# Row-tiled scores, a new beginning and copied global rows in a windowed attention with MLP

## The chip, the core and the metric

The kernel runs on one core of one Trainium2 chip. The metric is device time in microseconds of one execution; the profile beside it comes from one profiled execution of the same program. The engines are called by the profile's short names: PE (TensorE, with PEld for its weight loads), DVE (VectorE), ACT (ScalarE), POOL (GpSimd) and SP (SyncE, here a queue of transfers).

## The reference

Eight batches of eight heads, 576 positions, head size 64. A query sees the keys within 32 positions of its own, and eight positions are global: they see all keys, and all queries see them. The result of the attention, laid out as 4608 tokens of 512, goes through an MLP with h times cos(h) between its two matrices.

```python
scores = scale * np.matmul(q, k.transpose(0, 1, 3, 2))
mask = np.abs(pos[:, None] - pos[None, :]) <= window        # window = 32
mask = mask | is_global[:, None] | is_global[None, :]
scores = np.where(mask, scores, -1000000000.0)
attn = np.exp(scores - np.max(scores, axis=-1, keepdims=True))
attn = attn / (np.sum(attn, axis=-1, keepdims=True) + 1e-09)
attn_out = np.matmul(attn, v)
x = attn_out.transpose(0, 2, 1, 3).reshape(B * S, H * D)     # 4608 x 512
h = x @ w_in                                                 # w_in 512 x 2048
out = (h * np.cos(h)) @ w_out                                # w_out 2048 x 512
```

## The kernel before

**Tiling.** The attention works on pairs of heads: 32 pairs, four to a batch. The 576 queries of a pair are cut into 11 blocks (`NB`) of 56 (`QB`). For a block the kernel holds 128 keys in `kw`: the 8 global ones in rows 0 to 7 and a window of 120 local ones; and 64 queries in `qb`: the 8 global ones and the block's 56. Head 0 of the pair lies in partitions 0 to 63, head 1 in 64 to 127. In `qb` each head has a slot of its own, zero in the other head's partitions, so that one matmul over all 128 partitions gives both heads' scores side by side.

The steps of a pair, by the letters with which the program writes its order:

- `k`, `q` (`local_k`, `local_q`): bring keys and queries into `kw` and `qb`. For the first eight pairs PE turns them from rows (`turned`, L492), and ACT and DVE copy them out of PSUM (L499, L512); from pair 8 on they come turned by a transfer from an fp16 copy in DRAM, and DVE lays them out (L502, L515).
- `g` (`globals_k`, `globals_q`): POOL copies the global keys and queries in (L479, L483, L484). They come from `kgT` and `qgT`, made at the start from gathered rows (`gather`, `build_globals`, L442, L464, L465).
- `s` (`scores`, L525 to L528), in three groups of 4, 4 and 3 blocks: matmuls `st`, exp on ACT to `e`, product with the mask on DVE to `pm`.
- `w` (`spread`, L370, L374, L377), first eight pairs only: PE spreads rows of v over the blocks' windows by matmuls with shifted identities (`shift`), and the global rows of v with `own`; each block takes its global rows first, then one or two shifted parts. ACT and DVE copy the result to `vw`. Later pairs get `vw` from transfers (`load_v`, `load_vg`). `C` (`cast_vn`, L348 to L351) casts half a batch of v's rows to fp16 before its two pairs are spread.
- `p` (`values`, L537 to L548): 22 matmuls into one PSUM tile `pv`, then reciprocals of the denominators and the product `xn` on DVE.
- `x` (`turn_x`, L560 to L568): six transposes, and copies into `xT`, the MLP's input; with the last pair of a batch POOL puts the global queries' rows in place.

The MLP runs in units: `1` is one `ph` (four matmuls of 512 columns, L578), its cos on ACT (L584) and its product g on DVE (L585); `2` is four matmuls of 512 columns into `po` (L595), four of which make an output tile that ACT or DVE copies out. `m` is the matmul part of a `1` alone, `t` its ACT and DVE part. `n` (L614) sums squares for a check, on ACT.

**Order.** All engines work in program order, and the order is written out by hand. First comes a straight beginning (memsets, index rows, masks, the loads of the first q and k). Then `FRONT` runs pairs 0 to 7 with hardly any MLP. Then 13 turns (s = 3 to 15) do the attention of two pairs (`a`, `z`) beside eight `1` and eight `2`, after `ORDER`, with `MID` in place of it in the first turn and small variants in the next three. A tail does the rest of the MLP. Letters `L`, `W`, `O`, `K`, `B`, `A`, `c` issue transfers: halves of q and k, w_in, w_out, fp16 copies, turned q and k with v, the later gathers, v's fp16 copy.

**Queues.** POOL issues the loads that change type (q, k, w_in, w_out, fp16 copies) and the gathers; SP issues v's rows (24 loads by `load_vn`), the turning transfers, `load_v`, `load_vg`, the later gathers and the output.

**PSUM.** Eight banks: `s` three (scores, spread, and outside the front the transposes of x), `h` two (ph; in the front the turned q and k), `o` one (po; in the front the transposes of x), `pv` two. A wait for a bank is a wait for the last reader of what was in it.

Of the kernel before, what the change touches and what calls it, by code (L numbers as in the profile page):

```python
# [19 lines left out]
P = 128  # L20
# [20 lines left out]
ORDER = "sa0 sa1 sa2 2 2 2 sz0 2 sz1 sz2 pa 1 1 2 xa pz G 1 1 2 xz n 1 1 2 kc qc 1 kd qd 2 1"  # L41
# [3 lines left out]
FOURTH = "2 2 sa0 sa1 sa2 2 sz0 2 sz1 sz2 pa 1 1 2 xa pz G 1 1 2 xz n 1 1 2 kc qc 1 kd qd 2 1"  # L45

FIFTH = "sa0 sa1 sa2 2 2 2 sz0 2 sz1 sz2 pa 1 2 xa pz G 1 2 xz n 1 2 kc qc 1 kd qd 2"

SIXTH = "sa0 sa1 sa2 2 2 2 sz0 2 sz1 sz2 pa 1 1 2 xa pz G 1 1 2 xz n 1 1 D0 2 kc qc D1 1 kd qd D2 2 1"

FRONT = ("s0.0 s0.1 s0.2 k1 q1 C0 w0 s1.0 s1.1 s1.2 L2 p0 k2 q2 C1 w1 x0 s2.0 s2.1 s2.2 W0 p1 k3 q3 C2 w2 x1 "
         "s3.0 s3.1 s3.2 L3 W1 A g4 g5 p2 k4 q4 w3 x2 s4.0 s4.1 s4.2 g6 g7 c4 K4 W2 W3 p3 k5 q5 C3 w4 x3 s5.0 s5.1 s5.2 p4 k6 q6 w5 x4 n0 "
         "s6.0 s6.1 s6.2 K5 p5 k7 q7 w6 x5 B4 s7.0 s7.1 s7.2 O p6 w7 n1 x6 m p7 m x7 t t")
# [145 lines left out]
def kernel(  # L199
# [51 lines left out]
    qb = [keep.tile([P, 2, NB, C], FP16, name=f"qb{i}") for i in range(NK)]  # L251
# [33 lines left out]
    d_i = keep.tile([P, C], I32)  # L285

# [37 lines left out]
    shift = xT[:, 0, 4 * TT : 5 * TT].rearrange("p (a n) -> p a n", n=P)  # L324
    own = xT[:, 1, 4 * TT : 6 * TT].rearrange("p (a n) -> p a n", n=P)
# [13 lines left out]
    def hold(pr):  # L339

        nc.gpsimd.tensor_copy(gate, qb[pr % NK][0:1, 0, 0, G : G + 1])
# [11 lines left out]
    def build_shifts():  # L353
# [5 lines left out]
        nc.vector.tensor_copy(own[:, :, 0:G], ident16[:, 0 : 8 * G].rearrange("p (b g) -> p b g", g=G))  # L359

    def spread(pr):

        new, h0 = vn16(pr // 2), 2 * (pr % 2) * D
        for g0 in range(0, NB, 4):
            n = min(4, NB - g0)
            t = ps.tile([P, 4, P], FP32, tag="s", bufs=3)
            for j in range(g0, g0 + n):
                i = j // 2
                parts = ((2, i), (3, i + 1)) if j % 2 else ((0, i), (1, i - 1))
                nc.tensor.matmul(t[:, j - g0], own[:, pr], vg16[:, 0].rearrange("p h d -> p (h d)"), start=True, stop=False)  # L370
                parts = [(a, x) for a, x in parts if x >= 0]
# [14 lines left out]
    mask = keep.tile([P, NB, 2, C], FP16)  # L386

    def build_mask():
# [26 lines left out]
        for h in range(2):  # L415
            nc.vector.tensor_tensor(
                mask[:, :, h, G:], view(nk, (1, NB), (0, QB)), view(band[:, G:], (0, NB), (1, QB)), ALU.mult)
            nc.vector.tensor_scalar(
                mask[:, :, h, 0:G], view(val, (1, NB), (0, G)), own[:, 0:1], None, ALU.mult)
# [11 lines left out]
        for h in range(2):  # L431
            nc.vector.tensor_copy(mask[0:G, :, h, G:], view(one, (0, NB), (0, QB)))
# [5 lines left out]
    def build_globals(half):  # L438
        both = []
        for src, dst in ((kg32, kgT), (qg32, qgT)):  # L440
            g16 = work.tile([P, P], FP16, tag="g16")
            nc.scalar.copy(g16, src[:, half].rearrange("x h d -> x (h d)"))  # L442
# [422 lines left out]
```

## Time and profile before

| | us |
|---|---|
| median of 3 runs | 369.73 |
| range of the runs | 367.13 to 370.02 |
| the profiled execution: its own time | 371.58 |
| the profiled execution: span from first to last instruction | 369.8 |

Mean granted PE clock over the span 0.988. Busy shares of the span: PE 91%, PEld 50%, DVE 72%, ACT 67%, POOL 29%.

A row of the profile names the source line, the engine, the operation, output and inputs, the shape, and how many there were; then busy time and mean duration of one, and the idle time just before it with what ended it. The chain of waits follows the work that ended last back through whatever released it; "issue" there is time in which an engine waited for nothing that the profile shows. Starts of matmuls in a row overlap their ends, so the distance from one group's start to the next one's start is the time that a group costs PE, and not its printed duration.

### The profile page before, as it was taken

What the parts mean: (1) busy time and instruction counts of PE and PEld (TensorE: products, weight loads), DVE (VectorE), ACT (ScalarE), POOL (GpSimd) and SP (SyncE); (2) the same over time, 40 slices, a digit from 0 to 9 for tenths busy, and PEclk for the clock granted to TensorE, in tenths of its full rate; (3) what the DMA queues carried; (4) which work ended last, traced back from release to release, by engine and by line L of the source; (5) the groups of instructions that cost most, each with busy time, mean ns of one, the idle gap of its engine ahead of it and who ended that gap; (6) DMA issues with size and microseconds to landing.
All of it is one profiled execution on the core that took longest, in us unless ns stands there. A gap on an engine that the chain in (4) does not pass through costs nothing.

```text
span 369.8 us, 8014 instructions
## 1 busy us (share of the span) xinstructions
PE 335.9 (91%) x2934; PEld 184.9 (50%) x2934; DVE 266.3 (72%) x615; ACT 249.5 (67%) x384; POOL 105.9 (29%) x239
## 2 busy tenths in 40 slices
PE   0399883999998999999999999999999999999992
PEld 0277673545553545555555555555555444444441
DVE  7659974696888888888888888888878445455410
ACT  5488882679776677778777868677787756644300
POOL 6735670161335250705253252603000100000000
PEclk9999997899999999999999999999999999999999
DMA  5979999999999999999999999999920000100111
GB/s 92 197 129 159 180 165 107 198 176 147 102 161 105 194 126 195 125 169 138 195 161 159 160 142 165 160 202 118 130 59 31 28 30 28 57 30 28 53 64 65
DMA packets 176280, 45.57 MB, mean 123 GB/s; under 512 B 164937, under 2 KB 171337, under 8 KB 176041
## 3 DMA queue, kind: packets, MB, share of 16 engines
q1 hardware_dynamic: 112601, 27.61, 58.3%
q0 software_dynamic: 63632, 17.37, 50.3%
q8 instruction: 25, 0.41, 0.5%
q14 instruction: 22, 0.18, 0.2%
HBM read 45.07 MB, written 20.05 MB: 176 GB/s over the span
## 4 chain that ended last, share of the span: by engine, by line
PE 79%; DVE 6%; issue 5%; ACT 3%; POOL 3%; DMA 2%; POOLq 0%; ACTq 0%
PE po L595 32%; PE ph L578 30%; PE st L525 5%; PE pv L537 4%; PE tx L560 2%; PE t L374 2%; DMA qn<-in_q_dram 2%; DVE g L585 2%; ACT e L527 1%; PE t L370 1%; PE t L492 1%; PE pn L628 1%; DVE xn L548 1%; POOL q L262 1%; ACT qb L512 1%
## 5 line engine op out<-in xcount | busy, mean ns | idle before, releaser
L584 ACT ACTIVATE cos<-ph,pio 128x512 f16<-128x512 f32 x144 | 97.1, 687 | 66.3 <-PE ph L578 64.7
L595 PE MATMUL po<-w_out,g 128*128 128x512 f16 x576 | 141.6, 379 | 0.0
L578 PE MATMUL ph<-xT,w_in 128*128 128x512 f16 x576 | 140.1, 379 | 0.3 <-DVE g L585 0.2
L585 DVE TENSOR_TENSOR g<-cos,ph 128x512 f16<-128x512 f16 x144 | 95.9, 685 | 46.9 <-ACT cos L584 44.9
L595 PEld LDWEIGHTS <-g 128*128 128x128 f16 x576 | 55.2, 98 | 62.1
L578 PEld LDWEIGHTS <-w_in 128*128 128x128 f16 x576 | 53.6, 98 | 60.5 <-issue 1.3
L527 ACT ACTIVATE e<-st 128x512 f16<-128x512 f32 (+1 forms) x96 | 47.9, 561 | 15.5 <-PE st L525 9.4
L528 DVE TENSOR_TENSOR pm<-e,mask 128x512 f16<-128x512 f16 (+1 forms) x96 | 37.2, 405 | 22.8 <-ACT e L527 21.0
L752 POOL COPY gate<-xn 1x1 f16<-1x1 f16 x12 | 2.2, 181 | 132.3 <-DVE xn L548 132.3
L525 PE MATMUL st<-qb,kw 128*128 128x128 f16 x352 | 29.2, 223 | 9.4 <-issue 5.0
L525 PEld LDWEIGHTS <-kw 128*128 128x128 f16 x352 | 24.1, 100 | 19.8 <-issue 9.1
L548 DVE TENSOR_TENSOR xn<-pv,r_all 128x768 f16<-128x768 f32 x32 | 30.7, 958 | 1.7
L568 POOL COPY xT<-xg 128x4 f16 x64 | 19.6, 306 | 28.7 <-DVE xT L563 25.3
L262 POOL DMA_DIRECT2D q<-in_q_dram x12 | 26.2, 2181 | 0.0
L614 ACT ACTIVATE sq<-xn 128x1536 f16<-128x1536 f16 x16 | 23.6, 1476 | 0.0
L515 DVE COPY qb<-qT 64x616 f16<-64x616 f16 x48 | 22.1, 460 | 0.3
L374 PE MATMUL t<-xT 112*128 112x128 f16 (+1 forms) x168 | 21.1, 240 | 0.7 <-ACT xT L349 0.4
L600 ACT COPY o<-po 128x512 f32<-128x512 f32 x18 | 10.5, 586 | 15.5 <-PE po L595 15.1
L262 POOL DMA_DIRECT2D k<-in_k_dram x12 | 19.8, 1646 | 0.0
L370 PE MATMUL t<-vg,xT 128*128 128x128 f16 x88 | 18.4, 242 | 0.9 <-issue 0.6
L537 PE MATMUL pv<-vw,pm 128*64 128x65 f16 x704 | 18.5, 199 | 0.0
L602 DVE COPY o<-po 128x512 f32<-128x512 f32 x18 | 12.3, 685 | 6.9 <-PE po L595 6.9
(123 smaller groups left out, 326.8 us busy)
## 6 DMA issues: line engine op xcount, KB each, us to landing
out_dram<-o SPq DMA_DIRECT2D x36, 256.0 KB
vw<-v SPq DMA_DIRECT2D x35, 165.0 KB
v<-in_v_dram POOLq DMA_DIRECT2D x12, 288.0 KB, 4.3
k<-in_k_dram POOLq DMA_DIRECT2D x12, 288.0 KB, 9.2
q<-in_q_dram POOLq DMA_DIRECT2D x12, 288.0 KB, 15.8
vn<-in_v_dram SPq DMA_DIRECT2D x20, 112.0 KB
w_in<-in_moe_w_in_dram POOLq DMA_DIRECT2D x4, 512.0 KB, 12.3
w_out<-in_moe_w_out_dram POOLq DMA_DIRECT2D x1, 2048.0 KB
```

What stands on the lines that cost most here:

```text
L262: nc.gpsimd.dma_start(dst[s].rearrange("t (h d) -> t h d", h=4), dview(src, base, (D, S), (S * D, 4), (1, D)))
L374: nc.tensor.matmul(t[:, j - g0], shift[0:m, a], new[0:m, x, h0 : h0 + 2 * D], start=False, stop=(a, x) == parts[-1])
L525: nc.tensor.matmul(st[:, j], kp[:, g0 + j], view(qp[:, :, g0 + j], (NB * C, 2), (1, C)), start=True, stop=True)
L527: nc.scalar.activation(e[:, :n], st[:, :n], AF.Exp, scale=scale)
L528: nc.vector.tensor_tensor(view(pm[:, g0], (1, n * P)), view(e, (1, n * P)), view(mask[:, g0], (1, n * P)), ALU.mult)
L537: nc.tensor.matmul(pv[r0 : r0 + C, j // 6, c0 : c0 + 65], pm[:, j, h], vp[:, j, h], start=True, stop=True)
L548: nc.vector.tensor_tensor(view(xn, (384, 2), (D, 6), (1, D)), view(pv, (512, 2), (65, 6), (1, D)), view(rp, (6, 2), (1, 6), (0, D)), ALU.mult)
L578: nc.tensor.matmul(ph, w_in16[:, j, f * P : (f + 1) * P], xT[:, j, t * TT : (t + 1) * TT], start=(j == 0), stop=(j == NC - 1))
L584: nc.scalar.activation(cos, ph, AF.Sin, bias=pio2)
L585: nc.vector.tensor_tensor(g, cos, ph, ALU.mult)
L595: nc.tensor.matmul(po, g16[:, f, s * P : (s + 1) * P], w_out16[:, f], start=(f == 0), stop=(f == NF - 1))
L614: nc.scalar.activation(sq, view(xn, (1, 2 * BP * P)), AF.Square, accum_out=x_sq[:, s : s + 1])
```

## The change

What it does:

- **Scores in row tiles.** `qb` loses its two zero-padded slots and holds both heads in their own partitions. Each block takes two matmuls, one on partitions 0 to 63 and one on 64 to 127, of 64 columns each, in alternation, into two PSUM banks. A whole pair is one step: blocks 0 to 7 of the two heads go into two banks, blocks 8 to 10 into two more; of the four, three have tag `s` and one `h` (in the front `o`). There are four exps (512, 512, 192, 192 columns) and three mask products. `pm` and the mask are laid out by head, and the mask has one copy for both heads. In the orders `sa0 sa1 sa2` become `sa`, and the second pair's groups, which stood around the fourth `2`, become one `sz` behind it.
- **Values.** The 22 matmuls alternate between the two column halves at every step.
- **Local queries** are copied by one instruction over 128 partitions instead of two over 64: in the front on ACT for pair 0 and odd pairs, on DVE for the others.
- **Beginning.** For pairs 0 and 1 the global keys and queries come from matmuls of the loaded rows with one-hot columns (`build_ones`, `pick_globals`), copied by ACT; the gathered rows of q and k are turned later, in two steps `H`. `warm` issues 7, 2 and 2 matmuls of identity with identity. Half of the memsets of the first k and q tiles move from DVE to ACT; v's rows are loaded only after a DVE memset that follows the index work; v's gather and the second load of q and k are issued before the gathers of k and q; `cast_vn(0)` moves into the beginning, ahead of the first scores; the memsets of `pv`, `kT` and `qT` come behind it.
- **Global rows of v.** For pairs 2 to 7 transfers copy them into spare rows of the tiles that get spread (`load_rows`), where the shifted identities have eight more rows for them; only pairs 0 and 1 still use `own`, once per group of blocks. Blocks that take the same shift go in one matmul of several columns' width.
- **Front.** Its steps are reordered, four units of ph are done in it instead of two, some with a third bank, and the transposes of x use tag `s`.

The core of the diff:

```diff
-ORDER = "sa0 sa1 sa2 2 2 2 sz0 2 sz1 sz2 pa 1 1 2 xa pz G 1 1 2 xz n 1 1 2 kc qc 1 kd qd 2 1"
+ORDER = "sa 2 2 2 2 sz pa 1 1 2 xa pz G 1 1 2 xz n 1 1 2 kc qc 1 kd qd 2 1"
...
+FRONT = ("s0 k1 i1 q1 j1 L2 w0 s1 k2 H0 C1 w1 H1 g2 g3 q2 p0 s2 W0 k3 q3 x0 C2 w2 p1 s3 L3 W1 A g4 g5 k4 q4 x1 w3 p2 "
+         "s4 g6 g7 c4 K4 W2 W3 k5 q5 x2 C3 w4 p3 s5 k6 q6 x3 w5 p4 s6 K5 k7 q7 x4 w6 p5 s7 B4 O w7 x5 n0 p6 + m m x6 p7 t t m m x7 t t n1 -")
+WARM = (7, 2, 2)
...
+    def build_ones():
+        gl = view(gidx_all, (0, RW), (2, G))
+        nc.vector.tensor_tensor(one_q, view(tok_i, (1, RW), (0, G)), gl, ALU.is_equal)
+        nc.vector.scalar_tensor_tensor(one_k, view(tok_i, (1, RW), (0, G)), float(-KPAD * RW), gl, ALU.add, ALU.is_equal)
+
+    def pick_globals(pr, src, ones, n, to):
+        t = ps.tile([P, G], FP32, tag="s", bufs=3)
+        for r in range(RW):
+            for h in range(2):
+                nc.tensor.matmul(t[h * D : (h + 1) * D], src[:n, 2 * pr + h, r], ones[:n, r], start=r == 0, stop=r == RW - 1)
+        nc.scalar.copy(to[:, :, 0:G], view(t, (0, NB), (1, G)))
+
+    def warm(n):
+        t = ps.tile([P, 4, P], FP32, tag="s", bufs=3)
+        for _ in range(n):
+            nc.tensor.matmul(t, ident16, view(ident16, (0, 4), (1, P)), start=True, stop=True)
...
+    def load_rows(s):
+        for pr in (2 * s, 2 * s + 1):
+            h0 = 2 * (pr % 2) * D
+            nc.sync.dma_start(vn16(s)[VT : VT + G, 0 : NVT - 1, h0 : h0 + 2 * D],
+                              view(vg16[pr * G : (pr + 1) * G, 0], (0, NVT - 1), (1, 2 * D)))
...
     def spread(pr):
...
-                nc.tensor.matmul(t[:, j - g0], own[:, pr], vg16[:, 0].rearrange("p h d -> p (h d)"), start=True, stop=False)
-                for a, x in parts:
-                    m = min(VT, S - VT * x)
-                    nc.tensor.matmul(t[:, j - g0], shift[0:m, a], new[0:m, x, h0 : h0 + 2 * D],
-                                     start=False, stop=(a, x) == parts[-1])
...
+            for n0, (a, j, k, x) in enumerate(runs):
+                m = min(VT, S - VT * x)
+                if m == VT and a in (0, 2, 4) and not first:
+                    m += G
+                nc.tensor.matmul(view(t[:, j], (2 * P, k), (1, P)), shift[0:m, a], new[0:m, x : x + k, h0 : h0 + 2 * D],
+                                 start=n0 == 0 and not first, stop=n0 == len(runs) - 1, skip_group_check=True)
...
-    def scores(pr, g):
-        for j in range(n):
-            nc.tensor.matmul(st[:, j], kp[:, g0 + j], view(qp[:, :, g0 + j], (NB * C, 2), (1, C)), start=True, stop=True)
...
+    def scores(pr):
+        kp, qp = kw[pr % NK], qb[pr % NK]
+        pm = pm_of[pr] = work.tile([P, 2, NB, C], FP16, tag="pm", name="pm")
+        tags = (("s", 3), ("s", 3), ("s", 3), ("o", 1) if front[0] else ("h", 2))
+        st = [ps.tile([P, 512], FP32, tag=tag, bufs=bufs, name="st") for tag, bufs in tags]
+        for j in range(NB):
+            for h in range(2):
+                hp = slice(h * D, (h + 1) * D)
+                nc.tensor.matmul(st[j // 8 * 2 + h][:, j % 8 * C : j % 8 * C + C], kp[hp, j], qp[hp, j], start=True, stop=True)
         for h in range(2):
+            e = work.tile([P, 512], FP16, tag="e", bufs=3)
+            nc.scalar.activation(e, st[h], AF.Exp, scale=scale)
+            nc.vector.tensor_tensor(view(pm[:, h], (1, 512)), e, view(mask, (1, 512)), ALU.mult)
+        e = work.tile([P, 512], FP16, tag="e", bufs=3)
+        n = (NB - 8) * C
+        for h in range(2):
+            nc.scalar.activation(e[:, h * n : (h + 1) * n], st[2 + h][:, 0:n], AF.Exp, scale=scale)
+        nc.vector.tensor_tensor(view(pm[:, 0, 8], (NB * C, 2), (1, n)), view(e, (n, 2), (1, n)), view(mask[:, 8], (0, 2), (1, n)), ALU.mult)
...
+        nc.scalar.activation(x_sq[:, 0:1], pio2, AF.Exp)
+        index_rows()
+        build_ones()
+        nc.vector.memset(vn32[0][0:1, 0, 0:1], 0.0)
         for s in range(2 * SB):
             load_vn(s)
+        gather(v, vg32, 0)
+        load_qk(1)
         gather(k, kg32, 0)
         gather(q, qg32, 0)
-        gather(v, vg32, 0)
...
+        warm(WARM[0])
         local_k(0)
+        pick_globals(0, kn[0], one_k, KP, kw[0])
+        warm(WARM[1])
         local_q(0)
-        build_globals(0)
+        pick_globals(0, qn[0], one_q, QP, qb[0])
         nc.scalar.copy(vg16[:, 0], vg32[:, 0])
-        for pr in range(4):
-            globals_k(pr)
-            globals_q(pr)
+        for s in range(1, 2 * SB):
+            load_rows(s)
+        cast_vn(0)
+        warm(WARM[2])
```

More of the change, by code (lines that the diff above doesn't have):

```diff
@@ L250 @@
     kw = [keep.tile([P, NB, P], FP16, name=f"kw{i}") for i in range(NK)]
-    qb = [keep.tile([P, 2, NB, C], FP16, name=f"qb{i}") for i in range(NK)]
+    qb = [keep.tile([P, NB, C], FP16, name=f"qb{i}") for i in range(NK)]
     def cast_half(s, which):
@@ L383, in load_vg @@
                 view(vg16[(pr % 16) * G : (pr % 16 + 1) * G, pr // 16, h], (0, NB), (1, D)))
-    mask = keep.tile([P, NB, 2, C], FP16)
+    mask = keep.tile([P, NB, C], FP16)
     def build_mask():
```

145 lines of the change are left out of this document (73 added, 72 removed).

## The prediction

> **What bounds the kernel now.** I read first the page's slices, then busy time by stage.
>
> ```profile
> PE   0399883999998999999999999999999999999992
> DVE  7659974696888888888888888888878445455410
> 56.00:64.00 8.00, 2.54 (x39) 2.04 (x39) 2.68 (x6) 2.06 (x5) 0.00 (x0) 0.80 1.66 103
> 72.00:80.00 8.00, 7.94 (x38) 3.52 (x36) 7.89 (x17) 5.63 (x9) 4.38 (x17) 1.00 1.37 194
> 150.00:200.00 50.00, 50.00 (x419) 26.69 (x418) 42.71 (x99) 38.00 (x58) 19.60 (x46) 1.00 1.61 163
> ```
>
> The columns of the last three are window, length, PE, PEld, DVE, ACT, POOL, clock, DMA share, GB/s. From 72 us on PE never rests (50.00 of 50.00), so there only its own work counts; before that it is idle a good part of the time, most of all at 56 to 64. The kernel is thus a front of 72 us with other limits, and a PE-bound rest. Next the chain of waits at that hole, and PE's timeline in one turn of the steady loop (start, us):
>
> ```profile
> 56.92 0.33 PE st L525 x3
> 57.25 5.04 issue
> 62.29 1.01 PE st L525 x8
> ```
>
> ```profile
> 158.00 0.39 PE L525 MATMUL st<-qb,kw 128*128 128x128 f16 x4
> ...
> 159.09 0.55 PE L525 MATMUL st<-qb,kw 128*128 128x128 f16 x7
> 159.57 0.57 PE L537 MATMUL pv<-vw,pm 128*64 128x65 f16 x22
> 160.07 1.90 PE L578 MATMUL ph<-xT,w_in 128*128 128x512 f16 x8
> ...
> 171.72 0.78 PE L525 MATMUL st<-qb,kw 128*128 128x128 f16 x11
> 172.33 0.59 PE L595 MATMUL po<-w_out,g 128*128 128x512 f16 x2
> ```
>
> In the hole PE stops in the middle of the 11 matmuls of one step and waits for nothing recorded; the DMA share is 1.66, and one 16 KB instruction fetch lies in it. Last the engines' rows by form (count, busy us, mean ns):
>
> ```profile
> L527 ACT ACTIVATE e<-st 128x512 f16<-128x512 f32 x64 | 36.0, 596 | 15.5 <-PE st L525 9.4 <-DVE pm L528 5.9
> L527 ACT ACTIVATE e<-st 128x384 f16<-128x384 f32 x32 | 15.8, 492 | 0.0
> L515 DVE COPY qb<-qT 64x616 f16<-64x616 f16 x48 | 22.1, 460 | 0.3
> L512 DVE COPY qb<-t 64x616 f16<-64x616 f16 x7 | 5.6, 803 | 1.6 <-ACT qb L512 1.5
> ```
>
> **The steady loop (13 turns of 16.92 us).** A turn is 8 ph and 8 po groups (0.863 each: 13.8), 22 score blocks, two value steps, two transposes. Eleven blocks take 172.33-171.72 = 0.61, so 55.6 ns a block. New are 22 matmuls of 64 columns, two per block in the two row halves. If halves overlap, a block takes half, 28 ns: 0.31 a step; if not, 0.61 as now. No row shows row halves, but the column halves of the value step are near: 22 matmuls of 65 columns in 160.07-159.57 = 0.50, the change to ph included, 23 ns each, where one alone needs 28. They overlap, so I take 0.32 and save 0.29 a step, 0.58 a turn.
>
> Against it: changing the shape of the tile costs time. From the seven st to pv are 0.48, seven blocks are 0.39, so 0.09. The scores now have a shape of their own: into and out of the first score step, and into the second (its way out is a change already): 3 x 0.09 = 0.27 back. PE nets -0.3 a turn. The new order in the value step saves nothing: its halves overlap now.
>
> What is late next: the scores take four PSUM banks, one of them from ph's two, and the second step's 11 blocks all stand behind the fourth po, where four stood before it. From the rows, exps are 0.49 apart at 512 columns and (596-492)/128 = 0.8 ns a column cheaper below, so 512, 512, 192, 192 spread over 0.49+0.49+0.23+0.34 = 1.55 from the step's first 16 matmuls. Laid out over a turn: two changes, 0.32 and four po put the second step at 4.06; its exps run from 4.42 to 5.97 (now, by the same layout, to 5.62), so the mask products end at 6.35, reciprocals and xn at 7.81; the table load (1.28) ends at 7.2 and cos and g follow every 0.6. The second ph would start at 5.83 and waits for the bank of the last exp, 0.16; the first transpose would start at 7.71 and waits for xn, 0.11; a later ph, at 11.67, waits for a g that DVE had to put behind the second xn, 0.17: +0.44. The same layout of the kernel before gives no wait, as the trace has it. DVE gives back one 0.46 copy a step (128x616 at once), which is cover only. Turn: 16.92-0.30+0.44, about 17.0, so +1.1 over 13 turns. Ends: no stall, -3.9; no overlap, where the same layout gives 17.53, +8.
>
> **The front.** From s2 (28.76) to s7 (56.92) a pair takes 5.63, with 0.96 and 0.59 of empty PE waits in these five. Sums per pair: DVE 1.23 masks, 1.53 reciprocals and xn, 0.80 q copy, 0.69 vw, 0.67 turned x, 0.44 cast: 5.36. ACT 1.47 exps, 1.26 k copy, 0.67 q copy, 1.07 vw, 0.31 cast: 4.78. PE about 4.4, of which spread takes 36.41 to 38.61, 2.2 for 32 matmuls. So DVE leads. The transfers do not: from 24 to 26 us the queues are nearly empty, since the third k, q load waits for PE (24.91), and in the steady loop PE never waits for one.
>
> Spread sheds its 11 matmuls of globals (but for one per group in two pairs) and runs its 21 others as 14 longer ones: 21 x 0.056 = 1.2. PE falls to about 3.3 a pair, but it isn't the limit: what counts is the q copy, one of 128x616 at the same 0.80 or 0.67, on DVE in three pairs of eight and on ACT in five. DVE 4.87, ACT 4.61 plus the early globals; I take 5.0 a pair.
>
> Start: DVE sheds one mask half (0.82+0.26+0.46), the two qb memsets (1.3) and half of kn's and qn's (0.9), and gains about 1.2 of one-hot and shift building; its mask is ready near 12 rather than 13, which hides under v's rows. Now s0 runs at 16.72, behind gathers, casts and POOL's copies, and s1 at 23.89, slowed by a cold PE (11 blocks in 1.17 at 16.72: 106 ns each). After, k and q load without the v loads beside them (those wait for DVE's index work, about 5.9, instead of 2.57), one-hot matmuls replace the gathers on this path, and identity matmuls (11 x 0.43 cold, under the wait for kn) warm PE. But the cast of v's first half now stands in ACT's and DVE's queues ahead of the first exps, and with it everything waits for v's rows. Now they are last seen needed at 19.13; six loads started 3 us later with less beside them I put at 16, between 12 and 20. Behind it on ACT: cast 0.62, exps 1.55, k copy 1.26, pick 0.27, q copy 0.67, pick 0.27 = 4.6, so s1 near 21. POOL now issues v's gather and the second k, q load first, and SP's queue gains six small copies ahead of the late gathers; first use is 10 us on, cost nothing, 0.5 each if that cover goes.
>
> Then six pairs of 5.0 bring s7 to 51. From s7 to the last turned x are now 72.45-56.92-5.04 = 10.5 without the hole; after, 1.6 of cold spread goes and two more ph groups (1.7) come in, so 61.5. Empty waits for instructions were 6.6 in all (5.04, 0.96, 0.59); the number of PE instructions is about the same, w_out is still loading, so I keep 3 (0 to 7): 64.5. Against 72.45: -8; and two ph groups less are left for later: -1.7.
>
> **Sum.** -8-1.7+1.1 = -8.6. The profiled execution took 371.58 around its span of 369.8: 363.0; it lay 1.85 over the median of 369.73, so 361.
>
> **Rivals.**
> 1. Everything pays (22%): v's rows at 13 (-3), no new instruction wait (-3), no stall in the loop (-3.9 instead of +1.1): 350 to 356, 353. For it: 0.44 of stalls hangs on margins of 0.1 to 0.4.
> 2. Row halves don't overlap (11%): 28 ns a matmul, turn 17.53, +8 instead of +1: 368. No row here excludes it. The Trainium skill, "TensorE: Matmul & The Clock Gate", section "Wait — 56ns, not 53.3ns?", says that matmul starts never come closer than about 25 ns; by that figure a step would take 0.55 and the sum would be about 367. The trace speaks against it: the value step has 22 in 0.50 with a change of shape in it, and the turns of k and q show 31 in 0.59, 19 ns each.
> 3. The front doesn't shrink (7%): v's rows at 19 again, and an instruction wait of 5 or more with w_out: -2-1.7+1.1, 367 to 370, 369.
> 4. Slower (8%): a row half's weights (still 128 columns) occupy PE as long as a whole block does now, and the halves' loads don't overlap: 55.6 ns a matmul, 1.22 a step, +0.61 twice, 0.27 and 0.2 of waits, 1.7 a turn, +22: 382. For it: PEld of L525 shows 100 ns a load; against: value loads hide at 23 ns each. It decides from about 37 ns a matmul: at 28 the kernel stands at 368, and each ns adds 44 x 13 = 0.57.
>
> **How the numbers follow.** Forecast 52%, 361, itself 355 to 367. 1% is 3.7 us, about what a measurement here tells from no change: faster is under 366.0, slower over 373.4. Faster: 48 of the 52, 22, 3 of rival 2, 1 of rival 3: 74%. Same: 4, 7, 5: 16%. Slower: 8, and 1 each of rivals 2 and 3: 10%. The range runs from 351 (a third of rival 1 outside) to 369 (rival 4, half of 3 and some of 2 outside).
>
> **What would show it.** Steady turn: score steps in about 0.32 plus 0.09 at each end, turn 16.7 to 17.1; over 17.4 means no overlap. Front: s1 near 21, pairs near 5.0, first stretch of unbroken ph near 64; the first cast of v waiting for a DMA. The number is wrong if one instruction wait in the front exceeds 7 us, or if ph shows waits over 0.6 a turn.

## The result, and the profile after

| | before | after |
|---|---|---|
| median of 14 runs each, us | 368.6 | 374.31 |
| range, us | 365.71 to 374.67 | 370.92 to 377.56 |
| profiled execution: own time / span, us | 371.58 / 369.8 | 374.67 / 373.0 |
| mean granted PE clock | 0.988 | 0.968 |

The ratio of after to before is 1.0139, 95% interval 1.011 to 1.0169: the change makes the kernel 1.4% slower, where a gain of 2.3% was forecast. In the profiled executions it is 3.2 us of span against a forecast of -8.6. Ratios, here and below, are of the fast executions of both kernels (those within 1.5% of a kernel's fastest), so they can differ from the quotient of the medians by up to 0.9%.

First the page's slices of PE and its clock (9.3 us each), which answer to the first fence of the prediction:

```profile
PE   4884989769998999999999999999999999999992
...
PEclk9995799969999999999999999999999999999998
```

Before, there was one gap, in the seventh slice (56 to 65 us). Now there are two: in the fourth slice (28 to 37) and in the eighth and ninth (65 to 84), where before no gap was. The windows (window, length, then busy time and count of PE, PEld, DVE, ACT, POOL, then clock, DMA share, GB/s) give their size:

```profile
24.00:32.00 8.00, 3.46 (x101) 2.60 (x100) 5.21 (x14) 5.80 (x14) 5.26 (x14) 0.75 0.82 156
32.00:40.00 8.00, 5.81 (x94) 4.47 (x95) 2.85 (x8) 2.76 (x7) 1.37 (x4) 0.50 1.00 163
72.00:80.00 8.00, 2.52 (x8) 0.80 (x7) 3.18 (x7) 1.29 (x3) 0.28 (x2) 0.73 1.26 194
80.00:88.00 8.00, 8.00 (x32) 3.37 (x32) 4.81 (x8) 5.87 (x9) 4.55 (x7) 0.84 1.55 131
150.00:200.00 50.00, 49.72 (x487) 24.45 (x486) 39.77 (x89) 38.32 (x62) 18.06 (x39) 1.00 1.55 166
```

At 72 to 80 us PE was busy for 7.94 of 8 before, and is for 2.52 now. After each gap PE also runs cold: its granted clock is 0.50 at 32 to 40 and 0.84 at 80 to 88. PE's waits name what ended the two gaps, 5.0 and 5.3 us (engine, line, releaser, total, times, longest; the 5.1 behind the identity lies at the very start, when there is nothing else to do):

```profile
PE ph L621 <- DVE g L628: 5.3, 1, 5.3
PE t L308 <- POOL ident L748: 5.1, 1, 5.1
PE t L415 <- DMA xT<-vg: 5.0, 1, 5.0
```

The first is the third pair's spread, which waits for the copied global rows. The second looks like a wait for DVE, but the chain of waits (start, us, what) shows what DVE stood behind: the copy of the first transposed q.

```profile
57.09 2.49 SPq L274
...
59.68 17.11 DMA qT<-q
76.82 0.47 DVE qb L552
77.30 1.19 DVE g L628 x2
```

Both come from SP. Its timeline, here of after:

```profile
5.58 22.46 SPq L357 DMA_DIRECT2D vn<-in_v_dram  x24
28.16 4.51 SPq L391 DMA_DIRECT2D xT<-vg  x6
38.05 6.33 SPq L814 DMA_DIRECT2D kg<-in_k_dram  x8
...
57.09 2.49 SPq L274 DMA_TRANSPOSE kT<-k  x1
59.68 5.91 SPq L275 DMA_TRANSPOSE qT<-q  x1
```

and of before:

```profile
2.57 20.12 SPq L334 DMA_DIRECT2D vn<-in_v_dram  x24
27.78 6.25 SPq L764 DMA_DIRECT2D kg<-in_k_dram  x8
...
48.23 1.98 SPq L274 DMA_TRANSPOSE kT<-k  x1
```

The six new copies stand behind all 24 loads of v's rows, which begin 3.0 us later; so they go out at 28 to 32.7, and the third pair waits for them until 34.19. Everything behind them on SP, the 24 late gathers and then the transposes, is 9 to 10 us later than before (38.05 against 27.78, 57.09 against 48.23). The q transpose was asked for at 59.68 and was needed at 70.8.

The loop, in PE's timeline over one turn (start, us):

```profile
156.21 0.49 PE L562 MATMUL st<-qb,kw 64*128 64x64 f16 x22
156.63 3.63 PE L638 MATMUL po<-w_out,g 128*128 128x512 f16 x16
160.19 0.49 PE L562 MATMUL st<-qb,kw 64*128 64x64 f16 x22
160.62 0.56 PE L580 MATMUL pv<-vw,pm 128*64 128x65 f16 x22
161.12 2.12 PE L621 MATMUL ph<-xT,w_in 128*128 128x512 f16 x8
163.08 1.03 PE L638 MATMUL po<-w_out,g 128*128 128x512 f16 x4
...
172.39 1.03 PE L621 MATMUL ph<-xT,w_in 128*128 128x512 f16 x4
173.35 0.49 PE L562 MATMUL st<-qb,kw 64*128 64x64 f16 x22
```

A turn is 173.35-156.21 = 17.14 where it was 16.92. A score step now takes 0.42 to 0.43 from its first start to the next group's, the change of shape behind it included, where it took 0.61; the change into it adds about 0.1 (172.39 to 173.35 is 0.96 for four ph matmuls, 0.86 where no score step follows). But ph's eight matmuls print 2.12 instead of 1.90: the second unit waits for its bank.

### The profile page after: what moved, and what is told of

The parts are those of the page before. It is cut to its first block, busy times and chain, and to the rows that moved or that the text cites. A ratio compares the mean times of both kernels' runs of the same rounds, so it can differ in the third digit from the quotient of the medians.

```text
span 373.0 us, 8565 instructions
## 1 busy us (share of the span) xinstructions
PE 341.3 (92%) x3223; PEld 172.3 (46%) x3223; DVE 251.8 (68%) x589; ACT 248.4 (67%) x416; POOL 94.0 (25%) x204
## 4 chain that ended last, share of the span: by engine, by line
PE 66%; SPq 14%; DMA 7%; issue 4%; ACT 4%; DVE 2%; POOL 1%; ACTq 0%; POOLq 0%
PE po L638 31%; PE ph L621 27%; SPq L357 6%; DMA qT<-q 5%; SPq L814 4%; PE tx L603 3%; PE st L562 2%; ACT e L565 2%; PE pv L580 2%; DMA vn<-in_v_dram 2%; SPq L422 1%; ACT e L570 1%; DVE g L628 1%; DMA vw<-vg 1%; SPq L809 1%
## 5 line engine op out<-in xcount | busy, mean ns | idle before, releaser
L621 PE MATMUL ph<-xT,w_in 128*128 128x512 f16 x576 | 143.7, 384 | 6.3 <-DVE g L628 5.3
L638 PE MATMUL po<-w_out,g 128*128 128x512 f16 x576 | 139.7, 380 | 0.2 <-ACT o L643 0.2
L565 ACT ACTIVATE e<-st 128x512 f16<-128x512 f32 x64 | 34.7, 594 | 13.5 <-PE st L562 13.1
L566 DVE TENSOR_TENSOR pm<-e,mask 128x512 f16<-128x512 f16 x64 | 26.6, 424 | 19.9 <-ACT e L565 18.4
L415 PE MATMUL t<-xT 120*128 120x256 f16 (+3 forms) x112 | 17.5, 284 | 6.6 <-DMA xT<-vg 5.0
L603 PE MATMUL tx<-ident,xn 128*128 128x128 f16 x192 | 16.8, 226 | 2.5 <-DVE xn L591 2.2
L562 PEld LDWEIGHTS <-kw 64*128 64x128 f16 x704 | 13.1, 97 | 12.7 <-issue 8.8
L520 POOL COPY kw<-kgT 128x88 f16<-128x88 f16 x30 | 14.7, 671 | 14.8 <-ACT kgT L506 8.1
L562 PE MATMUL st<-qb,kw 64*128 64x64 f16 x704 | 17.3, 195 | 0.9 <-DVE qb L549 0.6
L603 PEld LDWEIGHTS <-xn 128*128 128x128 f16 x192 | 12.1, 100 | 12.7 <-DVE xn L591 10.3
```

The source lines that it names most:

```text
L562: nc.tensor.matmul(st[j // 8 * 2 + h][:, j % 8 * C : j % 8 * C + C], kp[hp, j], qp[hp, j], start=True, stop=True)
L565: nc.scalar.activation(e, st[h], AF.Exp, scale=scale)
L566: nc.vector.tensor_tensor(view(pm[:, h], (1, 512)), e, view(mask, (1, 512)), ALU.mult)
L603: nc.tensor.transpose(tx[:, n], xn[:, n], ident16)
L621: nc.tensor.matmul(ph, w_in16[:, j, f * P : (f + 1) * P], xT[:, j, t * TT : (t + 1) * TT], start=(j == 0), stop=(j == NC - 1))
L638: nc.tensor.matmul(po, g16[:, f, s * P : (s + 1) * P], w_out16[:, f], start=(f == 0), stop=(f == NF - 1))
```

## The experiments

Two theories. **T1**: the front lost on SP: the late copies make the first hole, the late gathers the second, and the loop loses only what the second score step costs by its late place. **T2**, the rival: the front has reached another limit (DVE, the DMA engines, PE's instructions), and what one hole gives back appears in the next place. All ratios are to the kernel before on the same chip, with their 95% intervals. The kernel before has medians from 368.6 to 371.4 on the chips used, so differences of under 1% between rows of this table are weak evidence; the marks of the profiled executions say more. "First po" is where the first matmul of the second MLP half starts (before 87.78, after 90.10), a mark for the end of the front. In the recorded expectations s0 to s7 are the score steps of the front's eight pairs, and pn is the first matmul of a check behind the loop.

| run | median, us | ratio | first po, us | steady turn, us |
|---|---|---|---|---|
| after | 374.31 | 1.0139 (1.011 to 1.0169) | 90.10 | 17.14 |
| rows_early | 370.83 | 0.9993 (0.9951 to 1.0035) | 88.32 | 17.14 |
| turn_first | 367.93 | 0.9948 (0.9905 to 0.9992) | 78.79 | 17.14 |
| rows_and_turn | 367.0 | 0.9912 (0.9879 to 0.9944) | 77.78 | 17.14 |
| sz_earlier | 370.24 | 0.9958 (0.9917 to 0.9999) | 88.55 | 16.90 |
| row_scores_alone | 370.27 | 1.0022 (0.9983 to 1.006) | 87.12 | 17.14 |
| rows_by_matmul | 369.41 | 0.995 (0.9895 to 1.0005) | 79.68 | 17.14 |
| gathers_late_alone | 379.9 (four runs, 373.57 to 382.58) | no interval | 79.99 | 17.14 |
| all_mended | 378.76 | 1.023 (1.018 to 1.0279) | 78.51 | 16.90 |
| no_warm | 373.34 | 1.0187 (1.0088 to 1.0285) | 90.01 | 17.14 |
| gathers_on_pool | 371.44 | 1.0108 (1.0001 to 1.0215) | 87.39 | 17.14 |
| all_on_pool | 364.64 | 0.9924 (0.988 to 0.9968) | 83.95 | 16.91 |
| all_by_matmul | 366.0 | 0.9925 (0.9872 to 0.9978) | 84.16 | 16.91 |
| pool_gathers_in_middle | 361.08 | 0.9771 (0.9706 to 0.9836) | 79.58 | 16.90 |
| pool_gathers_early | 361.34 | 0.9812 (0.9757 to 0.9867) | 79.45 | 16.90 |

**The copies ahead of half of v's loads (rows_early).**

```diff
-        for s in range(2 * SB):
+        for s in range(2):
             load_vn(s)
         gather(v, vg32, 0)
...
         for s in range(1, 2 * SB):
             load_rows(s)
+        for s in range(2, 2 * SB):
+            load_vn(s)
         cast_vn(0)
```

> The six small copies of global rows go into SP's queue ahead of the last 12 loads of v instead of behind all 24. Theory A (two holes in series on SP's queue: 5.0 us at 29 us, where the third pair's spread waits for the copies, and 5.3 us at 73 us, where the copy of the turned q waits for its transfer): the first hole goes, pairs 2 to 7 run about 5 to 7 us earlier, but the turned q still lands near 77, so the second hole grows to about 10 to 12 us and the time falls by less than 2 us. Rival B (the first hole alone is the loss): the time falls by 5 to 8 us. Rival C (the loop alone, 0.22 us more in each of 13 turns, is the loss, the holes being covered elsewhere): no change of the time and no new hole.

The first hole is gone: the fourth score step starts at 33.5 instead of 37.7. The second stays and grows, from 5.3 to 6.1, because the q transpose, asked for at 58.20, lands at 75.06. So the copies' rank in SP's queue makes the first hole. Its size is not fixed: with the copies where the change has them, the same wait is 3.0, 2.9 and 1.2 us in no_warm, gathers_on_pool and sz_earlier below, and none in turn_first and gathers_late_alone; they land just when they are due, and 5.0 is the dear end. None of the six profiles with the copies ahead of half the loads has the wait. From the third score step to the fourth is 4.83 here, and 10.69, 9.18, 8.39, 6.88, 6.05 and 4.83 in the six profiles with the change's order of copies and loads.

The expectation's sizes missed: the second hole was to grow to 10 to 12 and the time to fall by less than 2. The hole is 6.1, and the profiled span falls by 2.9, of which 1.8 is there at the first po. As sz_earlier, whose front is the change's own, reaches the first po 1.55 earlier than the change does, a mend of 1.8 there is not clear of the scatter between executions.

**The transposes ahead of the late gathers (turn_first).**

```diff
-... L3 W1 A g4 g5 ... c4 K4 W2 W3 ... s7 B4 O ...
+... L3 W1 g4 g5 ... c4 K4 T4 A W2 W3 ... s7 U4 O ...
+"T": turn_half, "U": lambda s: (load_values(2 * s), load_values(2 * s + 1)),
```

> The turning transfers of the fourth half go into SP's queue ahead of the 24 late gathers instead of behind them; the loads of v for pairs 8 and 9 stay where they were. Theory A: the turned q lands 8 us or more earlier, the hole at 73 us goes (5.3 us and some 2 us of cold clock behind it): 5 to 8 us less. Rival B: no change, since the hole at 29 us stays. Rival C: no change.

The transposes are asked for at 42.86, the second hole is gone, and the first po comes 11.3 us earlier than after the change. Of these, 4.0 are there at the eighth score step already (53.25 against 57.21), before the edit can act: this execution has no first hole. From the eighth score step to the first po are 25.54, where after the change has 32.89; so 7.3 are the edit's. The forecast of 5 to 8 us less held (367.93 against 374.31). But the gathers now stand ahead of the v tiles of the first late pairs, and the chain of waits has a new piece:

```profile
83.58 5.34 DMA vw<-vg
88.97 0.72 PE pv L580 x22
```

PE waits 3.0 us in all for such tiles, and the turns behind the front (from one first transpose of x to the next; the second one has less MLP in it) are 18.41, 13.15, 18.38 and 18.09 long, where after the change they are 17.15, 13.15, 17.74 and 18.05.

**Both together (rows_and_turn).** The two edits above in one kernel.

> Both edits. Theory A: both holes go, 10 to 14 us less than the changed kernel, so 6 to 10 us less than the kernel before: 359 to 363. Rival B: as rows_early alone. Rival C: no change.

First po 77.78, the earliest of all runs, and the same wait on the v tiles, 3.1 us. The time missed its forecast: 367.0 against 359 to 363, and not clearly better than turn_first alone (the intervals overlap). Neither place tried for the gathers on SP in the front, ahead of the transposes or behind them, is free: the holes follow SP's order, as T1 says, and a part of what they give back appears in the next place, as T2 says.

**The second score step one po group earlier (sz_earlier).**

```diff
-ORDER = "sa 2 2 2 2 sz pa 1 1 2 ...
+ORDER = "sa 2 2 2 sz 2 pa 1 1 2 ...
```

(and so in the three variants)

> The second score step of a turn goes one po group earlier (three po groups between the two score steps instead of four, one behind). Theory: PE's 0.49 us of waits a turn (second ph for the bank of the last exp 0.22, transpose for xn 0.20, later ph 0.07) come from the exps ending too late; they end about 0.75 us earlier, the waits go, a new one of up to 0.2 comes at the score banks: turn 16.75 to 16.9 instead of 17.14, 3 to 4.5 us less in all. Rival: the row tiles themselves cost PE more than they save (drains), then the turn stays at 17.1.

The turn falls from 17.14 to 16.90. The loop's loss was due to the place of the second score step, as expected; thirteen turns make 3.1 us (forecast 3 to 4.5). The second hole is there as after the change (7.2 us of PE's wait), so this edit leaves the front's loss as it was.

**The scores alone (row_scores_alone).** The kernel before with the row-tiled scores and all that hangs on them, its own beginning, gathers and spread:

```diff
-            nc.tensor.matmul(st[:, j], kp[:, g0 + j], view(qp[:, :, g0 + j], (NB * C, 2), (1, C)), start=True, stop=True)
+                nc.tensor.matmul(st[j // 8 * 2 + h][:, j % 8 * C : j % 8 * C + C], kp[hp, j], qp[hp, j], start=True, stop=True)
...
-FRONT = ("s0.0 s0.1 s0.2 k1 q1 C0 w0 s1.0 s1.1 s1.2 ...
+FRONT = ("s0 k1 q1 C0 w0 s1 ...
```

> The kernel before with the scores in row tiles alone (q tiles without the zero halves, one mask for both halves, the new order of the score steps and of the value step); beginning, gathers and spread as before. Theory: the turn is the changed kernel's, 17.14 (16.92 before), so +2.9 over 13 turns; the front's pairs lose one q copy and stay at 5.4 to 5.7 or fall to 5.2; first po within 2 of the 87.78 before; ratio 1.000 to 1.010. Rival: the turn's +0.22 comes from something else in the change, and the turn is 16.90 to 16.95 here.

Turn 17.14: the loop's loss belongs to the scores and to nothing else in the change. The front ends as before (87.12), so all the rest of the change's loss and all of its possible gain lie in the beginning, the spread and the front's order. The pairs of this front did not come as expected (5.2 to 5.7): from the third score step on they take 5.20, 5.13, 6.14, 7.45 and 7.98, with empty waits of PE of 0.72 and 2.10 inside two value steps, for which the profile names no cause.

**Global rows by matmuls for every pair (rows_by_matmul).**

```diff
-        first = pr < 2
+        first = True
...
-        for s in range(1, 2 * SB):
-            load_rows(s)
```

(with eight one-hot blocks in `own` again)

> The changed kernel without the copies of global rows by transfers: every pair adds them by a matmul with one-hot rows, as the first two pairs do (one matmul a group more, three a pair). Theory: the first hole (PE waiting for those copies, 5.0 at 29 to 34) is gone, s3 near 33 instead of 37.7, PE's longer spread costs a pair nothing; the second hole grows by what the first gives, because the transposes still stand behind the gathers; first po 87 to 90, ratio 0.998 to 1.010. Rival: the shorter spread carries the front, and the pairs from s3 to s7 take 5.3 or more instead of 4.9.

The first hole is gone, as both expected, and the pairs from the fourth score step to the eighth take 4.95 as with the copies (4.88): the shorter spread carries nothing that can be seen. What I had not expected is that the second hole is gone too. SP's timeline says why:

```profile
31.75 6.30 SPq L812 DMA_DIRECT2D kg<-in_k_dram  x8
...
51.60 2.21 SPq L274 DMA_TRANSPOSE kT<-k  x1
53.90 3.65 SPq L275 DMA_TRANSPOSE qT<-q  x1
```

Without six copies ahead of them the gathers start 6.3 us earlier, the transposes are asked for 5.5 earlier, and DVE copies the first transposed q at 67.67 with no wait. Its ten runs spread from 364.75 to 373.21 with a median of 369.41, so the profiled one, 364.75, is the fastest of them: the missing second hole is shown for that execution, and the others may have it.

**The gathers off the front, still on SP (gathers_late_alone, all_mended).** The first moves step `A` alone; the second also has the edits of rows_early, turn_first (without `A`) and sz_earlier.

```diff
-... s3 L3 W1 A g4 g5 k4 ...
+... s3 L3 W1 g4 g5 k4 ...
...
-MID = "+ 1 1 kc qc ... n2 1 1 1 1 1 1 -"
+MID = "+ 1 1 kc qc ... n2 1 1 1 1 1 A 1 -"
```

> The changed kernel with one step moved: the 24 late gathers go from the front to the middle block; the transposing transfers stay where they are in the order. Theory (the gathers keep SP from asking for the transposes): the transposes are asked for near 48 instead of 57.1 and landed by 68, PE's second hole (5.3 us at 72 to 78) is under 1.5, the first hole (5.0 at 29 to 34) stays, first po 84 to 86 against 90.10, turn 17.14; ratio 0.995 to 1.003, against 1.0139 for the changed kernel. Rival: the transposing transfer is slow by itself or waits for its cast, and the hole keeps 3 us or more.

> Four orders changed at once in the changed kernel: the last two sets of v loads behind the copies of the global rows; the transposing transfers of k and q asked for right behind their cast; the 24 late gathers moved from the front into the middle block, behind everything the front needs from SP; the second score step one po group earlier. Theory (SP's queue order made both holes, the late second score step made the loop's stall): neither hole is there, no PE wait on the v tiles of the first late pairs (3.0 a wait in the run with both earlier moves), first po group near 76, turn 16.90, first pn 286 to 291 against 294.00 with the first two moves alone; ratio to before 0.970 to 0.982. Rival A (the gathers only move their harm): the 24 gathers now stand ahead of the transfers of the following turns, a wait of 5 us or more in one of the first three turns, first pn 291 to 296, ratio 0.984 or more.

The second hole is gone from both, as forecast. The first po comes at 79.99 (forecast 84 to 86, with the first hole, which is not there either) and 78.51 (forecast near 76). The time did not come as forecast: all_mended's rival A was right. SP's timeline of gathers_late_alone, and PE's first wait behind it:

```profile
97.10 6.46 SPq L814 DMA_DIRECT2D kg<-in_k_dram  x8
...
109.58 6.00 SPq L814 DMA_DIRECT2D vg<-in_v_dram  x8
115.68 1.00 SPq L647 DMA_DIRECT2D out_dram<-o  x2
116.77 1.77 SPq L274 DMA_TRANSPOSE kT<-k  x1
```

```profile
122.83 0.77 PE L562 MATMUL st<-qb,kw 64*128 64x64 f16 x22 [12.68 <-DVE qb L552]
```

The transposes of the next half are asked for at 116.77; in rows_by_matmul, where nothing stands before them, at 97.49. PE waits 12.7 us (16.4 in all_mended) in one turn of 28.28 (31.76). The gathers cost SP 18.5 us of issuing (97.10 to 115.58) and, ahead of them, eight loads of row numbers into registers, some 4.6 us: more than a whole turn of 17 us.

**The gathers on POOL (gathers_on_pool, all_on_pool, all_by_matmul).** Six indexed gathers take the place of 24 copies; the second kernel adds the edits of rows_early and sz_earlier, the third those of rows_by_matmul and sz_earlier.

```diff
-            row = [nc.values_load(gidx_row[0:1, 2 * g : 2 * g + 1], engines=[mybir.EngineType.SP], ...
             for src, dst in ((k, kg32), (q, qg32), (v, vg32)):
-                late = src[B // 2 :].rearrange("b (n h) s d -> (b n) h s d", h=2)
-                for g in range(G):
-                    nc.sync.dma_start(dst[g:P:G, 1], late[...])
+                gather(src, dst, 1)
...
-... L3 W1 A g4 g5 ... s7 B4 O w7 ...
+... L3 W1 g4 g5 ... s7 B4 O A w7 ...
```

> The changed kernel with the 24 late gathers of SP replaced by 6 indexed gathers that POOL issues behind the load of w_out (POOL is idle from 58.7 to 67.4, and one such issue takes 0.95 to 1.44 in the start). Theory (SP's queue is the cause of the second hole, and no turn of the loop has room for these gathers on SP): the transposes are asked for at 45, the second hole goes, no turn is longer than 20, first po near 80 as in the run with the gathers in the middle block, first pn 291 to 295; ratio 0.980 to 0.995. Rival: the gathers' own traffic, not the queue they stand in, holds the transposes up, and 3 us or more of wait on q's copy stay; ratio over 1.0.

> The same, and two orders more: the last two sets of v loads behind the copies of the global rows, and the second score step one po group earlier. Theory: neither hole, turn 16.90, first po 76 to 79, first pn 285 to 290; ratio 0.968 to 0.982. Rival: DMA load holds the front anyway (share 1.0 to 1.9 in every stretch) and the wait comes back on another tile (v tiles, w_in or w_out); ratio 0.985 or more.

> As the run before this one, but with the global rows of every pair added by one-hot matmuls in place of the copies, and the v loads in the changed kernel's order. Theory (the copies cost more on SP than they save on PE): within 0.5% of the run before this one, on either side; ratio 0.968 to 0.985. Rival: the shorter spread is worth its copies once SP's order is right, 0.6 us in each of six pairs, and this run is 0.8% or more behind the other.

The transposes are asked for at 45.31 and the wait on q's copy is gone in all three; no turn is longer than 18.11. But the front does not end at 80: each of the three has a new hold at the seventh pair's transposes, 3.65, 2.93 and 4.42 us. So the queue was the cause of the second hole, as the theory said, but the forecast of the end of the front was wrong, and all three ratios lie outside those expected (all_on_pool's rival expected 0.985 or more, but from a wait on a transfer, and that is not what came). The timeline of all engines in gathers_on_pool:

```profile
59.64 0.57 PE L580 MATMUL pv<-vw,pm 128*64 128x65 f16 x22
...
60.14 1.90 PE L621 MATMUL ph<-xT,w_in 128*128 128x512 f16 x8
...
64.02 0.16 DVE L585 TENSOR_REDUCE dg<-pv 8x2 f32<-8x12 f32 x1 [3.68 <-remote]
...
65.46 0.69 ACT L627 ACTIVATE cos<-ph,pio 128x512 f16<-128x512 f32 x1 [2.90 <-remote]
65.69 0.82 PE L603 MATMUL tx<-ident,xn 128*128 128x128 f16 x6 [3.65 <-DVE xn L591]
```

PE's records go on to 62.04, but DVE, which needs only pv, starts at 64.02, and ACT, which needs only ph, at 65.46. PE's signal for pv comes at 64.00, 3.8 us after the printed end of its last matmul; in gathers_late_alone it comes 0.02 after it. So PE was held, and its printed ends are not the real ones there. The second and third kernels have ratios of 0.9924 and 0.9925, with intervals of half a per cent on either side: no difference between copies and one-hot matmuls shows here.

**What holds PE (pool_gathers_in_middle, pool_gathers_early).** all_on_pool with the six gathers elsewhere: behind the front, or ahead of the casts of k and q.

```diff
-... s7 B4 O A w7 ...
+... s7 B4 O w7 ...
-MID = "... n2 1 1 1 1 1 1 -"
+MID = "... n2 1 1 1 1 1 A 1 -"
```

```diff
-... L3 W1 g4 g5 k4 ... s7 B4 O A w7 ...
+... L3 W1 g4 g5 A k4 ... s7 B4 O w7 ...
```

> As the run with everything on POOL, but POOL issues the 6 gathers in the middle block, behind the front, where it is idle 5 to 11 us at a time. Theory (the hold of 2.9 to 4.4 us at PE's last transposes of the front comes with the gathers issued just then, together with the load of w_out): no hold there, first po 77.5 to 80.5 against 83.95, no turn over 20, first pn 287 to 290; ratio 0.975 to 0.987. Rival: the hold comes from w_out's load and PE's own instruction fetch beside it, as the 5.04 in the kernel before, and stays; first pn 292 to 295, ratio as the run with everything on POOL (0.9924).

> As before, with the 6 gathers issued by POOL near 31, ahead of the casts of k and q. Theory: no hold at the last transposes either; the casts behind the gathers on POOL are asked for 1 to 3 us later and the transposes with them, still in time; first po 77.5 to 81, ratio 0.975 to 0.988. Rival: the hold stays, or the casts are late and the wait on q's copy comes back, 2 us or more.

No hold in either; first po 79.58 and 79.45, ratios 0.9771 and 0.9812, both as forecast. In pool_gathers_early the transposes are asked for 3.4 us later than in pool_gathers_in_middle (49.15 against 45.73) and are still in time. The page's slices of PE for pool_gathers_in_middle:

```profile
PE   4697998999999899999999999999999999999993
```

Both holes are closed. POOL, which runs ahead of PE, issues the gathers from 74.75 to 82.4, and the longest wait left behind the front is 0.85 us, for a v tile:

```profile
118.40 0.78 PE L580 MATMUL pv<-vw,pm 128*64 128x65 f16 x22 [0.85 <-DMA vw<-vg]
```

The hold goes with the gathers' being issued right behind w_out's load, within 53 to 66 us: it is there in the three profiles with them at that place and in none of the others that have the change's front. By what way they hold PE is not settled, and gathers cannot be the only cause of such a thing: the kernel before was held for 5.04 us beside the same load with none issued there. The instruction fetches nearest to the three holds took 1.53, 0.92 and 1.05 us, against 2.36 in that hole of the kernel before, so a slow fetch does not show here.

The stretch from the eighth score step to the first po sums up the second hole and the hold over all 14 profiles with the change's front: 32.89 to 33.95 us in the four with the second hole (after, rows_early, sz_earlier, no_warm), 30.95 to 31.19 in the three with the hold, 25.54 to 26.39 in the seven with neither. The two kernels of this paragraph beat both the kernel before (by 2.3% and 1.9%) and the changed one.

**Without the identity matmuls (no_warm).**

```diff
-WARM = (7, 2, 2)
+WARM = (0, 0, 0)
```

> The changed kernel without its 11 identity matmuls in the beginning. Theory of the prediction (they lie under the wait for k and warm PE for the first two score steps): s0 and s1 later by 0.5 to 2, the first hole takes that up, since the third pair waits for copies by SP's clock, first po within 1 of 90.10; ratio 1.008 to 1.018. Rival: they stand in the way of the start, and s1 is earlier than 20.6 without them.

The first score step starts at 13.04 instead of 12.25, the second at 21.29 instead of 20.61, and the first po at 90.01. That looks like the 0.5 to 2 us of the expectation, but kernels with the same beginning and with the identity matmuls in it have the first step at 13.14 (sz_earlier), 13.06 (gathers_late_alone) and 13.04 (gathers_on_pool), and the second at 21.88, 21.75 and 21.43. So no help from the identity matmuls is shown. The holes are 3.0 and 6.9 us here, 5.0 and 5.3 after the change.

## Why the prediction was wrong

| mark | forecast | after | pool_gathers_in_middle |
|---|---|---|---|
| second score step, us | 21 | 20.6 | 20.5 |
| a pair in the front, us | 5.0 | 4.88 | 5.3 |
| eighth score step, us | 51 | 57.2 | 53.5 |
| last turned x, us | 64.5 | 67.4 | 64.1 |
| steady turn, us | 17.0 | 17.14 | 16.90 |
| time, us | 361 | 374.31 | 361.08 |

- **The score step** (0.32, and 0.09 for each change of shape): right. From the first to the last start of the 22 matmuls are 0.305 us, the way in costs 0.095 more than before, and PE's work per turn falls by 17.14-16.92-0.49 of waits = -0.27, forecast -0.30. Rivals 2 and 4 fall with it. The Trainium skill's floor of about 25 ns between starts ("TensorE: Matmul & The Clock Gate", section "Wait — 56ns, not 53.3ns?") does not hold across two row halves: 0.305/21 = 14.5 ns. Within one half it does, 11 starts at about 29 ns.
- **The stall in the loop** (0.44): right in kind and place. The second ph waits 0.225 (forecast 0.16), the first transpose 0.20 (0.11), a later ph 0.07 (0.17), 0.49 in sum. The turn was rounded down to 17.0 and is 17.14, so 13 turns cost 2.9 and not 1.1: a term under-sized by 1.8. sz_earlier shows that this was avoidable. (The layout's parts as named add up to 3.95 for the start of the second score step, 4.04 with the change of shape into it, where it says 4.06; the trace has 4.08, so nothing hangs on it.)
- **The start** (v's rows at 16, second score step near 21): right in time. The last cast of the first rows waited for them until 16.76. But it was not ACT's row of copies that set the second score step, as forecast: ACT was done with them at 18.15, and PE went on with the first pair's spread, which needs those rows, until 20.6. That the two ways come out alike is luck.
- **The pairs** (5.0 each): right in size for the four behind the first hole, 4.88 (4.9 to 5.6 in the other profiles); but between the third and the fourth score step lie 10.7. The reason given was wrong: DVE does not lead. The windows over the pairs, first of before, then of after, show it:

```profile
28.76:56.92 28.16, 24.13 (x515) 20.27 (x516) 24.81 (x62) 23.71 (x40) 17.99 (x32) 1.00 1.37 165
37.67:57.21 19.54, 17.45 (x386) 13.44 (x384) 16.48 (x44) 15.99 (x31) 10.82 (x19) 0.90 1.13 133
```

A pair keeps PE busy for 4.36 us after the change, at a granted clock of 0.90 (forecast 3.3), DVE for 4.12 (4.87) and ACT for 4.00 (4.61); before, PE had 4.83 (taken as 4.4) and DVE 4.96 (5.36 as the sum of its durations). So PE gave back 0.47 a pair and not 1.1, and it is now the busiest of the three; that 5.0 came out is partly luck.
- **The instruction waits** (3 us kept): the 5.04 of before is not there, and PE's waits name none for instructions at all; the 3 us are part of what the rest of the front did better.
- **The step that failed**: "SP's queue gains six small copies ahead of the late gathers; first use is 10 us on, cost nothing, 0.5 each if that cover goes", and with it "The transfers do not [lead]". The copies were costed against a first use 10 us on, and not against what stands ahead of them: 24 loads, which the same paragraph let start 3 us later. They went out from 28.16, and PE stood ready for them at 29.16. And what stands behind them, the 24 gathers and then the transposes, was not followed to its first use: before, the transposes were asked for at 48.23 and first used at 74.90; the first date moved 9 us later, and the second 4.6 earlier (70.32), 7.8 in pool_gathers_in_middle (67.15). The first hole cost 5.0, the second 5.3 and, by an estimate from the clock (8 us at 0.84), some 1.3 of cold PE behind it.
- **The sum.** The span missed by 11.8 us (373.0 against 369.8-8.6). Of it 5.3 and 1.3 are the second hole, 1.8 the loop, and 2.9 the last turned x at 67.4 instead of 64.5 (the first hole's 5.0, less 2.1 that the rest of the front did better); 0.5 is not placed.
- **The rivals**: none had this mechanism. Rival 3, a front that doesn't shrink, was the nearest in its effect; its causes, late rows of v and a wait for instructions, did not occur. Neither did the two signs that the prediction gave for a wrong number: no wait for instructions, and 0.30 of waits at ph in a turn.

That pool_gathers_in_middle comes to the forecast time is partly luck. It is not the change that was forecast: its gathers go by another queue in another form, the copies stand elsewhere, and its second score step comes one po group earlier. And its two parts differ from the forecast in opposite ways, a turn shorter by 0.1 and pairs longer by 0.3.

The Trainium skill, "DMA: Bandwidth & Descriptors", section "Issuing engines are not separate DMA queues", says that starting transfers from several engines saves only the time that a sequencer needs to start them, usually small beside the transfer itself. Here that time looks like most of the matter: with the gathers in the middle block, 23 us of SP's issuing there (94.66 to 117.68 in all_mended) against some 7.7 us of POOL's is 378.76 against 361.08 us in otherwise nearly equal kernels (the first also has turn_first's split of the transfers, and moves the rows by 24 copies where the second has six indexed gathers).

## What to carry to other kernels

Price a new transfer by its rank in the queue that issues it: what stands ahead (is it in time?), and what stands behind (follow each to its first use, with the dates of the faster kernel, since a front that gets faster needs its transfers earlier). A queue that is full in every turn has no place to hide a block of transfers; move the block to another issuer, and look again at what that one does beside it. A change that loses may be a good change with one order wrong: undo the waits one at a time before judging the idea.

## What the runs showed of the hardware

Matmuls in the two row halves start 14.5 ns apart on average: the second half's start comes 3 to 4 ns behind the first half's, and the next pair of starts mostly 25 or 26 ns later. A change of tile shape costs 0.10 us on the way into such a step and 0.12 on the way out.

The same transposing transfer, that of q, took 15.6 to 17.1 us from its issue to its landing in the front of the four profiles with the second hole (DMA share 1.4 to 1.5, with w_out's 2 MB and the fp16 copies beside it) and 3.55 us in the loop of gathers_late_alone (DMA share 1.13, PE idle). A cost per transfer read from one stage says little about another.

A matmul's printed end can be wrong by microseconds: in gathers_on_pool PE's signal came 3.8 us later. The Trainium skill, "Perfetto Trace Analysis", section "Tensor Engine Instruction (MATMUL, LD_WEIGHTS)", says that TensorE's end times are estimated and not observed; the trace agrees. Idle time of the engines that wait on PE is then the better witness. What held PE there, as what held it for 5.04 us at 57 us in the kernel before, stays open.
